# A transform-and-MLP kernel on one core: another order of loads, fillers and weight preparation in its opening

## The chip, the core and the metric

The kernel runs on one core of a Trainium2 chip. The core has a matrix engine (TensorE, PE; its weight loads are shown apart as PEld), a vector engine (VectorE, DVE), a scalar engine (ScalarE, ACT), a general engine (GpSimd, POOL) and a queue engine that only issues transfers (SyncE, SP). Transfers run on 16 DMA engines that SP, ACT and POOL feed through queues of their own. The metric is the device time of one execution in microseconds (us), the median over the runs.

## The reference

The input x has 8 entries of 3136 tokens of 256 features. Each entry is filtered along its tokens in the frequency domain, and each resulting token goes through a two-layer block with a softmax gate and a layer norm:

```python
X = np.fft.rfft(x, axis=1)                      # x: (8, 3136, 256)
y = np.fft.irfft(X * (filt_r + 1j * filt_i)[None], n=3136, axis=1)
x = y.reshape(25088, 256)
h = x @ w_in                                    # w_in: (256, 1024), float64 in memory
e = np.exp(h - h.max(-1, keepdims=True))
solu = h * (e / (e.sum(-1, keepdims=True) + 1e-09))
ln = (solu - solu.mean(-1, keepdims=True)) / np.sqrt(solu.var(-1, keepdims=True) + 1e-6) * g_ln
out = ln @ w_out                                # w_out: (1024, 256), float64 in memory
```

The two weights are float64 in memory; the kernel loads their words and turns them into float32 by integer operations.

## The kernel before

**The transform.** The 3136 tokens of an entry are 49 rows of 64. The transform along the 49 rows is a product with a small table (`first`, or `first_quarters` for later entries), in 8 pieces of 4 columns and their 4 mirror columns; then comes the transform along the 64 columns, the product with the filter, and the way back along the 64 columns, in 7 units (`forward`, `multiply`, `inverse`); then the way back along the rows (`back` for entry 0, `back_halves` for the others), which writes the tile `y` that the block reads. Entries 1 to 7 go through DRAM buffers `d1` and `d2` between these parts (`store_first`, `fetch`, `store`, `fetch_back`), and share the filter in `f_dram`.

**The opening.** Entry 0 stays on the chip. Its rows and mirrored rows are loaded into `rows_x` (L530): the first half of the partitions from SP, the second from POOL, with the four raw halves of `w_in` (`begin`, L521) between them on POOL's queue. SP then has the tables (L478), the filters (L485), small tables, six pieces of entry 1 (L473, into a part of `y` not yet used), the raw `w_out` (L425), and the stores of the filters to `f_dram` (L558). PE starts with 14 products that only keep it busy (`warm`), then 8 pieces of the row transform (L568), which ACT copies back to `rows_x` (L571). DVE converts three halves of `w_in` (`convert`, L444 to L458, nine instructions each), then turns the rows in place by four 32x32 transposes (`turn_rows`, L590). PE meanwhile does filler products (`idle`, L576) and turns the tables (`tables_back`, L498), and then the units run: `forward` on PE (L318), four multiplications on DVE (L339, L340), two additions on POOL (L341), a filler and `inverse` on PE (L576, L318), copies on ACT (L357). A second `turn_rows` follows, with six fillers beside it, then `back` (L410, copies on ACT L414), while DVE converts the last half of `w_in` and forms sums of weight blocks (`weight_sums`, L162).

**The steps.** After the opening the order is written out by hand, step after step: `step(k)` for k from 0 to 204, each with one half of a pair of 128-token blocks. A pair of blocks takes seven products with `w_in` (`product`, L755; a Strassen-like scheme over 2x2 blocks, whose sums POOL makes in `pair_sums`), which ACT and DVE bring out of PSUM (`keep`, L765; `finish`, L776 and L779), exponential, gate, turn and square (`exponential` L789, `normalize` L801, `turn` L819, `square` L809), and from step 9 on seven products with `w_out` (`project`, L891). Each engine does its instructions in the order in which they are written, so an instruction that waits holds up all that stands behind it on its engine. `PLAN` lists in which step each piece, unit and way back of entries 1 to 7 is done beside this:

```python
    ([0, 0, 0, 0, 1, 1, 1, 1], [4, 5, 6, 7, 8, 10, 12], [16, 17, 18, 19, 20, 20, 21, 22]),
```

is the line of entry 1: the first list gives the steps of its 8 pieces, the second those of its 7 units. At the end of a step come the preparation of `w_out` and the jobs in `late` and `loads`:

```python
        if k == 0:
            prepare_w_out(0)
        if k < 2:
            for n in range(2 * k, 2 * k + 2):
                convert_w_out(n)
        if k == 2:
            prepare_w_out(1)
        if k == 3:
            for n in range(2, 7):
                prepare_w_out(n)
```

`convert_w_out(n)` converts one quarter of `w_out` on DVE (nine instructions on 128x512) and scales it on ACT by `g_ln` (L682, four instructions). `prepare_w_out` takes the mean over the rows on PE (L700, 32 products), subtracts it on DVE (L705, 4) and forms the sums of blocks (L162, 4).

Of the kernel before, what the change touches and what calls it, by code (L numbers as in the profile page):

```python
# [52 lines left out]
def dft_tables():  # L53
# [19 lines left out]
    for a, part, sign in ((0, 0, 1), (1, 1, -1), (2, 1, 1), (3, 0, 1)):  # L73
# [18 lines left out]
    wb[:, :NK // 2] = wi[:, :, 0].reshape(NS, 2, 2, N1).transpose(2, 0, 1, 3).reshape(2, NK // 2, N1)  # L92
    wf0 = np.zeros((2, 64, 4, 32))
    wi0 = np.zeros((4, 32, NR))
    wf0[:, :N1, :, :NS] = wf.transpose(0, 1, 3, 2)
    wi0[:, :NS] = wi.reshape(NS, 4, NR).transpose(1, 0, 2)
    return wf.reshape(NR, NK).astype(f32), wf0.reshape(P, P).astype(f32), wq.reshape(P, 2, 64).astype(f32), \
        (-wi0).reshape(P, NR).astype(f32), (-wb).reshape(P, N1).astype(f32), de.astype(f32)
# [3 lines left out]
def kernel(  # L102
# [326 lines left out]
    with ExitStack() as st:  # L429
# [105 lines left out]
        wf0_t = fpool.tile([P, P], FP32, name="wf0_t", tag="wf0")  # L535
        nc.sync.dma_start(out=wf0_t, in_=wf0_dram)
        nc.scalar.dma_start(out=one, in_=one_dram)
        pieces = NH // NCH

        for i in range(pieces):  # L540
            fetch_x(0, NCH * i, NCH, 0, 64, nc.sync.dma_start)
            fetch_x(1, NCH * i, NCH, 0, 64, nc.gpsimd.dma_start if i else nc.scalar.dma_start)
            if i % 2:
                begin((0, 2, 1, 3)[i // 2], nc.gpsimd.dma_start)
        for load in (load_tables, load_filters):
            for i0, n in ((0, 4), (4, 4), (8, NP - 8)):
                load(i0, n, nc.sync.dma_start)
        nc.sync.dma_start(out=wi_t, in_=wi_dram)
        nc.sync.dma_start(out=wf_t, in_=wf_dram)
# [3 lines left out]
        fetch_second()  # L553
        for n in range(4):
            load_w_out(n, nc.sync.dma_start)
# [6 lines left out]
        for j in range(14):  # L562
            nc.tensor.matmul(out=ps_t.tile([P, P], FP32, name=f"warm_{j}", tag="t"), lhsT=one, rhs=one,
                             start=True, stop=True)
        for i in range(pieces):
            ps = ps_h.tile([P, 2, 512], FP32, name=f"pa_0_{i}", tag="h")
            for j in range(2):
                nc.tensor.matmul(out=ps[:, j], lhsT=wf0_t,  # L568
                                 rhs=rows_x[:, NCH * i + 2 * j:NCH * i + 2 * j + 2, :],
                                 start=True, stop=True)  # L570
            nc.scalar.copy(out=pairs_x[:, 2 * i:2 * i + 2].rearrange("p a c t -> p a t c"),  # L571
                           in_=ps.rearrange("p a (t c) -> p a t c", t=2))

        def idle(out):

            nc.tensor.matmul(out=out, lhsT=tables[0][0][:, 0, 0].rearrange("p u q -> p (u q)"),  # L576
                             rhs=filters[0][0][:, 0], start=True, stop=True)

        def idle_row(count, name):
            for j in range(count):  # L580
                idle(ps_h.tile([P, 2, C], FP32, name=f"{name}_{j}", tag="h"))

# [40 lines left out]
        turn_rows()  # L623
        convert(3)
# [50 lines left out]

    def convert_w_out(n):
        i, h, _ = quarters[n]
        power = pools["p"].tile([P, 512], I32, name=f"power_{n}", tag="pt")
        load_float64(w_out_sb[:, i].rearrange("p k d -> p (k d)"), raw_out[:, n], power)
        for f in range(KF // 2):  # L680
            fg = KF // 2 * h + f
            nc.scalar.activation(out=w_out_sb[:, i, f], in_=w_out_sb[:, i, f], func=AFT.Copy,  # L682
                                 scale=g_sb[:, fg:fg + 1])

    mean = {}

    def prepare_w_out(step):


        if step == 0:  # L690
            for name in ("ones", "w_bar"):
                mean[name] = pools["p"].tile([P, C], FP32, name=name, tag="pr" if name == "ones" else "pi")
            nc.vector.memset(mean["ones"][:, 0:P], 1.0)
            nc.vector.tensor_scalar(out=g_sb, in0=g_sb, scalar1=-1.0 / SHRINK, scalar2=None, op0=ALU.mult)
        elif step == 1:
# [239 lines left out]
    for e in range(1, B):  # L935
        first_at, spectrum_at, back_at = PLAN[e]
        sp = Spectrum(e, pools, load_filter, load_de)
        if e == 1:
            sp = second
            sp.load, sp.load_de = load_filter, load_de  # L940
        for i, t in enumerate(first_at):
            dma = nc.gpsimd.dma_start
            if e == 1:
# [56 lines left out]
    def step(k):  # L1000
# [94 lines left out]
        else:  # L1095
# [44 lines left out]
        for job in late[k] + loads[k]:  # L1140
            job()

    with tc.manual_schedule():
# [36 lines left out]
```

## Time and profile before

| what | value |
|---|---|
| median of 3 runs | 1608.41 us (1607.35 to 1610.21) |
| the profiled execution, its own time | 1609.97 us |
| its span in the profile | 1608.2 us |
| PE busy | 1555.3 us, 97% of the span |
| DVE busy | 1258.9 us, 78% |
| POOL busy | 1141.3 us, 71% |
| ACT busy | 924.7 us, 58% |
| data moved | 299.07 MB, mean 186 GB/s |

The span is the time from the first to the last instruction of the profiled execution; 1.8 us of its own time lie around it. A line of a timeline has the start, the duration, the engine, the source line, the operation with output and inputs, the count and, in brackets, how long the engine had been idle before it and what ended that. "PEq", "SPq" and the like are the sequencers that issue.

### The profile page before, as it was taken

The numbers are of one execution on the slowest core, as the hardware profiler recorded it, in microseconds if no ns is written. First come the engines' busy times: TensorE is split into PE (matmuls) and PEld (weight loads), VectorE is DVE, ScalarE is ACT, GpSimd is POOL, SyncE is SP. The second block draws the span as 40 slices with busy tenths as digits, with TensorE's granted clock in tenths as the row PEclk, the third lists the DMA queues.
The fourth block names the chain that finished last, engine by engine and source line by source line (L and its number), as shares of the span: only waits on it lengthen the run. The fifth ranks groups of instructions, "written<-read, shape, count | busy, mean of one in ns | idle before, by whom it ended". The sixth has DMA issues, their size and how long they took to land. (4 is left out here: it accounts for less than half of the span.)

```text
span 1608.2 us, 36683 instructions
## 1 busy us (share of the span) xinstructions
PE 1555.3 (97%) x12848; PEld 1066.7 (66%) x12848; DVE 1258.9 (78%) x2241; ACT 924.7 (58%) x1886; POOL 1141.3 (71%) x1338
## 2 busy tenths in 40 slices
PE   7976999999999999999999999999999999999997
PEld 3543466666666677667776677667766777777777
DVE  5655786898798888986888778986888777777773
ACT  2244565566565665665556655666656666666663
POOL 1432887679878877796788877697776766676765
PEclk8987999999999999999999999999999999999999
DMA  9624877887788678866897678766775454343444
GB/s 260 202 82 148 246 224 211 219 238 199 214 248 260 183 202 248 225 187 172 223 251 206 173 192 240 218 186 174 217 223 140 123 135 122 102 114 91 117 105 116
DMA packets 341128, 299.07 MB, mean 186 GB/s; under 512 B 28064, under 2 KB 310184, under 8 KB 340946
## 3 DMA queue, kind: packets, MB, share of 16 engines
q1 hardware_dynamic: 275026, 169.84, 39.9%
q0 software_dynamic: 31456, 93.53, 19.4%
q10 hardware_dynamic: 34464, 33.36, 7.1%
q8 instruction: 104, 1.70, 0.5%
q14 instruction: 78, 0.64, 0.1%
HBM read 119.02 MB, written 74.84 MB: 121 GB/s over the span
## 5 line engine op out<-in xcount | busy, mean ns | idle before, releaser
L891 PEld LDWEIGHTS o<-w_out_sb,solu_t 128*128 128x128 f32 x3136 | 382.7, 193 | 49.1 <-issue 43.5
L755 PE MATMUL m<-w_in_sb,s 128*128 128x512 f32 x784 | 402.0, 614 | 5.8 <-DVE nmax L779 3.4
L891 PE MATMUL o<-w_out_sb,solu_t 128*128 128x128 f32 x3136 | 401.6, 276 | 2.9 <-DVE ot L911 2.6
L891 PEld LDWEIGHTS o<-w_out_sb,u 128*128 128x128 f32 x2352 | 307.1, 192 | 138.4 <-issue 110.5
L891 PE MATMUL o<-w_out_sb,u 128*128 128x128 f32 x2352 | 310.9, 276 | 2.2 <-POOL u L734 1.6
L755 PE MATMUL m<-w_in_sb,y 128*128 128x512 f32 x588 | 308.5, 608 | 2.3 <-DVE h L776 2.3
L801 DVE SCALAR_TENSOR_TENSOR h<-e,h 128x1024 f32<-128x1024 f32 x196 | 307.8, 1570 | 0.0
L765 ACT COPY h<-m 128x512 f32<-128x512 f32 x294 | 173.0, 588 | 202.6 <-PE m L755 195.7
L907 ACT ACTIVATE ot<-o,rs_t 128x128 f32<-128x128 f32 x392 | 143.2, 367 | 245.7 <-PE o L891 244.1
L779 DVE CUSTOM_DVE_ANT_0 h<-m,h 128x512 f32<-128x512 f32 x196 | 134.3, 685 | 191.7 <-ACT h L765 112.7
L734 POOL TENSOR_TENSOR u<-solu_t 128x512 f32<-128x512 f32 x98 | 133.6, 1363 | 183.6 <-DMA solu_t<-turn 112.2
L809 ACT ACTIVATE h<-h,nmu 128x1024 f32<-128x1024 f32 x196 | 224.9, 1147 | 48.7 <-DVE turn L819 48.7
L819 DVE STREAM_TRANSPOSE turn<-h 128x1024 f32<-128x1024 f32 x196 | 243.1, 1240 | 3.1
L789 ACT ACTIVATE e<-h,nmax 128x1024 f32<-128x1024 f32 x196 | 225.3, 1149 | 6.9 <-DVE h L801 5.5
L734 POOL TENSOR_TENSOR u<-solu_t,u 128x512 f32<-128x512 f32 x98 | 136.0, 1388 | 93.8 <-PE o L891 93.5
L755 PEld LDWEIGHTS m<-w_in_sb,s 128*128 128x128 f32 x784 | 129.0, 192 | 93.5 <-issue 73.1
L911 DVE SCALAR_TENSOR_TENSOR ot<-o,rs_t,ot 128x128 f32<-128x128 f32 x299 | 103.7, 347 | 98.5 <-ACT ot L907 56.4
L734 POOL TENSOR_TENSOR u<-u,solu_t 128x512 f32<-128x512 f32 x98 | 160.2, 1634 | 15.2 <-PE o L891 8.3
L755 PEld LDWEIGHTS m<-w_in_sb,y 128*128 128x128 f32 x588 | 98.0, 193 | 97.5 <-issue 53.0
L734 POOL TENSOR_TENSOR solu_t<-solu_t,solu_t 128x512 f32<-128x512 f32 x98 | 156.1, 1593 | 0.9
L734 POOL TENSOR_TENSOR s<-y 128x128 f32<-128x128 f32 x196 | 96.2, 491 | 26.5 <-ACT y L414 26.0
L387 PEld LDWEIGHTS py<-wb_t,t 50*64 50x64 f32 x3584 | 57.6, 135 | 43.1 <-issue 18.7
(124 smaller groups left out, 1968.5 us busy)
## 6 DMA issues: line engine op xcount, KB each, us to landing
solu_t<-turn SPq DMA_DIRECT2D x780, 128.0 KB
out_dram<-ot SPq DMA_DIRECT2D x196, 128.0 KB
t<-d POOLq DMA_DIRECT2D x112, 200.0 KB, 6.8
d<-x POOLq DMA_DIRECT2D x100, 200.0 KB, 5.1
f<-f_dram POOLq DMA_DIRECT2D x39, 512.0 KB, 7.7
t<-d ACTq DMA_DIRECT2D x37, 512.0 KB
d<-g POOLq DMA_DIRECT2D x36, 512.0 KB, 5.1
x<-in_x_dram SPq DMA_DIRECT2D x112, 98.0 KB
```

What stands on the lines that cost most here:

```text
L387: nc.tensor.matmul(out=views[g][64 * h:64 * h + 64, cb, i, :], lhsT=t4[rows, i, c0:c0 + 64], rhs=wb_t[rows, 0:N1], start=True, stop=True)
L734: nc.gpsimd.tensor_tensor(out=out, in0=in0, in1=in1, op=op)
L755: nc.tensor.matmul(out=ms[j, bank], lhsT=lhsT, rhs=w_in_sb[:, w, :], start=m in (1, 2, 7), stop=True, skip_group_check=True)
L765: nc.scalar.copy(out=h_half(k, i), in_=ms[j, 0])
L779: nc.vector.tensor_tensor_reduce(out=h_half(k, i), in0=ms[j, bank], in1=h_half(*kept), scale=1.0, scalar=sofar, op0=ALU.add, op1=ALU.min, ...
L789: nc.scalar.activation(out=e, in_=hs[k], func=AFT.Exp, bias=nmaxs.pop(k)[:, 1:2], scale=-1.0, accum_out=esums[g][:, i:i + 1])
L801: nc.vector.scalar_tensor_tensor(out=solu, in0=e, scalar=SHRINK, in1=solu, op0=ALU.mult, op1=ALU.mult, accum_out=nmu)
L809: nc.scalar.activation(out=solu, in_=solu, func=AFT.Square, bias=nmu, scale=-float(DFF), accum_out=variances[g][:, i:i + 1])
L819: nc.vector.transpose(out=turns[g][:, :, i, :], in_=solus[k].rearrange("p (f j) -> p f j", j=32))
L891: nc.tensor.matmul(out=pos[p, bank], lhsT=lhs[:, f, :], rhs=w[:, f, :], start=f == 0 and (m in (1, 2, 7) or alone), stop=True, skip_group_ ...
L907: nc.scalar.activation(out=out_half(p, *to)[0], in_=pos[p, 0], func=AFT.Copy, scale=rs)
L911: nc.vector.scalar_tensor_tensor(out=ot, in0=pos[p, bank], scalar=rs, in1=out_half(p, *kept)[0], op0=ALU.mult, op1=ALU.add)
```

## The change

The opening and the first seven steps are put in another order; the computation is the same. The changed parts:

- The first table has 98 rows, not 128, and the rows of x stand on 98 partitions: 48 of the first half (SP), 49 of the second (POOL; its first piece is 48 rows and one more from ACT), and the 49th row of the first half apart, in two pieces. Before, 64 rows were loaded for each half.
- ACT's queue has the first piece of the second half and the raw halves 0 and 2 of `w_in`; halves 1 and 3 go to SP's queue behind the filters. Tables and filters alternate. The pieces of entry 1 come ahead of the small tables, the raw `w_out` behind the stores to `f_dram`. `one` goes to the end of POOL's queue.
- 10 `warm` products with the first table, not 14 with `one`. The fillers are 128x128 products of `one`: eight ahead of each group of tables. The fillers in the units and beside the second turn are gone.
- Only two halves of `w_in` are converted ahead of the first turn; the other two follow the second turn.
- The last unit's additions are on DVE, not POOL. The last copy of the row transform is made in two halves.
- Pieces 0 to 2 of entry 1 are done beside the second turn (`EARLY`), pieces 3 to 5 in step 0, and 6 and 7 in step 1.
- One quarter of `w_out` is converted in each of steps 0 to 3, in two halves of 128x256, and scaled by ACT one step later. The mean is in step 5, subtraction and sums in step 6; the two small tiles of the mean lie in `raw_out`.

```diff
+EARLY = 3
-    ([0, 0, 0, 0, 1, 1, 1, 1], [4, 5, 6, 7, 8, 10, 12], [16, 17, 18, 19, 20, 20, 21, 22]),
+    ([0] * 6 + [1] * 2, [4, 5, 6, 7, 8, 10, 12], [16, 17, 18, 19, 20, 20, 21, 22]),
...
-            dma(out=rows_x[64 * h + r0:64 * h + r0 + rows, n0:n0 + n],
+            to = NR - 1 if r0 else (N1 - 1) * h
+            dma(out=rows_x[to:to + rows, n0:n0 + n],
...
-        nc.scalar.dma_start(out=one, in_=one_dram)
+        fetch_x(1, 0, NCH, 0, N1 - 1, nc.scalar.dma_start)
+        fetch_x(0, 0, NH // 2, N1 - 1, 1, nc.scalar.dma_start)
+        nc.scalar.dma_start(
+            out=rows_x[NR - 2:NR - 1, 0:NCH][:, ::-1],
...
+        begin(0, nc.scalar.dma_start)
+        begin(2, nc.scalar.dma_start)
+        nc.scalar.copy(out=small_consts[:, 5:6], in_=small_consts[:, 0:1])
         for i in range(pieces):
-            fetch_x(0, NCH * i, NCH, 0, 64, nc.sync.dma_start)
-            fetch_x(1, NCH * i, NCH, 0, 64, nc.gpsimd.dma_start if i else nc.scalar.dma_start)
-            if i % 2:
-                begin((0, 2, 1, 3)[i // 2], nc.gpsimd.dma_start)
-        for load in (load_tables, load_filters):
-            for i0, n in ((0, 4), (4, 4), (8, NP - 8)):
+            fetch_x(0, NCH * i, NCH, 0, N1 - 1, nc.sync.dma_start)
+            if i == pieces // 2 - 1:
+                fetch_x(0, NH // 2, NH // 2, N1 - 1, 1, nc.sync.dma_start)
+            if i:
+                fetch_x(1, NCH * i, NCH, 0, N1, nc.gpsimd.dma_start)
+        nc.gpsimd.dma_start(out=one, in_=one_dram)
+        for i0, n in ((0, 4), (4, 4), (8, NP - 8)):
+            for load in (load_tables, load_filters):
                 load(i0, n, nc.sync.dma_start)
+        begin(1, nc.sync.dma_start)
+        begin(3, nc.sync.dma_start)
...
-        for j in (0, 2, 1):
+        for j in (0, 2):
             convert(j)
-        idle_row(3, "idle")
         for i0, n in ((0, 4), (4, 4), (8, NP - 8)):
+            idle_row(8, f"idle_{i0}")
             tables_back(i0, n)
-            idle_row(2, f"idle_{i0}")
         turn_rows()
...
-            sp.multiply(i, 0, nc.gpsimd.tensor_tensor)
-            sp.multiply(i, 1, nc.gpsimd.tensor_tensor)
+            add = (nc.gpsimd if i + 1 < units else nc.vector).tensor_tensor
+            sp.multiply(i, 0, add)
+            sp.multiply(i, 1, add)
...
-            idle(pss[0])
...
-        idle_row(6, "idler")
+        turn_rows()
+        for i in range(EARLY):
+            for u in range(2):
+                second.first(i, (u,), ps_t.tile([P, 2, C], FP32, name=f"pa_1_{i}_{u}", tag="t").rearrange(
...
+                second.store_first(i, 2 * u, nc.gpsimd.dma_start)
...
-        turn_rows()
+        convert(1)
         convert(3)
...
         if k == 0:
+            nc.vector.tensor_scalar(out=g_sb, in0=g_sb, scalar1=-1.0 / SHRINK, scalar2=None, op0=ALU.mult)
+        if k < 4:
+            for half in range(2):
+                convert_w_out(k, half)
+        if k == 4:
             prepare_w_out(0)
-        if k < 2:
-            for n in range(2 * k, 2 * k + 2):
-                convert_w_out(n)
-        if k == 2:
+        if k == 5:
             prepare_w_out(1)
-        if k == 3:
+        if k == 6:
             for n in range(2, 7):
                 prepare_w_out(n)
         for job in late[k] + loads[k]:
             job()
+        if 0 < k < 5:
+            scale_w_out(k - 1)
```

In the changed kernel the lines of the steps are some 22 higher: `product` is L777, `finish` L798 and L801, `project` L913, the row transform of entry 0 L582, its turn L605, `forward` and `inverse` L320, the conversions L446 to L460, the scaling L706.

More of the change, by code (lines that the diff above doesn't have):

```diff
@@ L92, in dft_tables @@
     wb[:, :NK // 2] = wi[:, :, 0].reshape(NS, 2, 2, N1).transpose(2, 0, 1, 3).reshape(2, NK // 2, N1)
[L93 removed]
+    wf0 = np.zeros((2, N1, 4, 32))
     wi0 = np.zeros((4, 32, NR))
[L95 removed]
+    wf0[:, :, :, :NS] = wf.transpose(0, 1, 3, 2)
+    wf0 = wf0.reshape(NR, P)[np.r_[0:N1 - 1, N1:NR, N1 - 1]]
     wi0[:, :NS] = wi.reshape(NS, 4, NR).transpose(1, 0, 2)
[L97 removed]
+    return wf.reshape(NR, NK).astype(f32), wf0.astype(f32), wq.reshape(P, 2, 64).astype(f32), \
         (-wi0).reshape(P, NR).astype(f32), (-wb).reshape(P, N1).astype(f32), de.astype(f32)
@@ L560 @@
                 in_=f[0:rows, at:at + n].rearrange("p i k c -> p i (k c)"))
-        for j in range(14):
-            nc.tensor.matmul(out=ps_t.tile([P, P], FP32, name=f"warm_{j}", tag="t"), lhsT=one, rhs=one,
+        for n in range(4):
+            load_w_out(n, nc.sync.dma_start)
+        for j in range(10):
+            nc.tensor.matmul(out=ps_t.tile([P, P], FP32, name=f"warm_{j}", tag="t"), lhsT=wf0_t, rhs=wf0_t,
                              start=True, stop=True)
@@ L568 @@
                 nc.tensor.matmul(out=ps[:, j], lhsT=wf0_t,
-                                 rhs=rows_x[:, NCH * i + 2 * j:NCH * i + 2 * j + 2, :],
+                                 rhs=rows_x[0:NR, NCH * i + 2 * j:NCH * i + 2 * j + 2, :],
                                  start=True, stop=True)
-            nc.scalar.copy(out=pairs_x[:, 2 * i:2 * i + 2].rearrange("p a c t -> p a t c"),
-                           in_=ps.rearrange("p a (t c) -> p a t c", t=2))
+            size = 2 if i < pieces - 1 else 1
+            for j in range(0, 2, size):
+                nc.scalar.copy(out=pairs_x[:, 2 * i + j:2 * i + j + size].rearrange("p a c t -> p a t c"),
+                               in_=ps[:, j:j + size].rearrange("p a (t c) -> p a t c", t=2))
         def idle(out):
-            nc.tensor.matmul(out=out, lhsT=tables[0][0][:, 0, 0].rearrange("p u q -> p (u q)"),
-                             rhs=filters[0][0][:, 0], start=True, stop=True)
+            nc.tensor.matmul(out=out, lhsT=one, rhs=one, start=True, stop=True)
         def idle_row(count, name):
             for j in range(count):
-                idle(ps_h.tile([P, 2, C], FP32, name=f"{name}_{j}", tag="h"))
+                idle(ps_h.tile([P, P], FP32, name=f"{name}_{j}", tag="h"))
         def convert(j):
@@ L674, in load_filter, with convert_w_out, scale_w_out @@
         return f
-    def convert_w_out(n):
+    def convert_w_out(n, half):
+        i = quarters[n][0]
+        part = slice(256 * half, 256 * half + 256)
+        power = pools["p"].tile([P, 256], I32, name=f"power_{n}_{half}", tag="pt")
+        load_float64(w_out_sb[:, i].rearrange("p k d -> p (k d)")[:, part], raw_out[:, n, part], power)
+    def scale_w_out(n):
         i, h, _ = quarters[n]
-        power = pools["p"].tile([P, 512], I32, name=f"power_{n}", tag="pt")
-        load_float64(w_out_sb[:, i].rearrange("p k d -> p (k d)"), raw_out[:, n], power)
         for f in range(KF // 2):
@@ L683, in convert_w_out @@
                                  scale=g_sb[:, fg:fg + 1])
-    mean = {}
+    mean = {name: raw_out[:, n].rearrange("p k w -> p (k w)").bitcast(FP32)[:, 0:C]
+            for n, name in enumerate(("ones", "w_bar"))}
     def prepare_w_out(step):
         if step == 0:
-            for name in ("ones", "w_bar"):
-                mean[name] = pools["p"].tile([P, C], FP32, name=name, tag="pr" if name == "ones" else "pi")
             nc.vector.memset(mean["ones"][:, 0:P], 1.0)
-            nc.vector.tensor_scalar(out=g_sb, in0=g_sb, scalar1=-1.0 / SHRINK, scalar2=None, op0=ALU.mult)
         elif step == 1:
@@ L941 @@
         for i, t in enumerate(first_at):
+            if e == 1 and i < EARLY:
+                continue
             dma = nc.gpsimd.dma_start
```

12 lines of the change are left out of this document (7 added, 5 removed).

## The prediction

> **What bounds the kernel now.** I read the page's slices first, then the busy time of each engine by stage, then the timeline of the stages that are not full.
>
> The slices (40.2 us each; tenths of PE's busy time and of its granted clock):
>
> ```profile
> PE   7976999999999999999999999999999999999997
> PEclk8987999999999999999999999999999999999999
> ```
>
> PE has holes only in the first four slices. The stage view (edges chosen at: turn starts, first forward matmul, units done, step 0, step 4, step 9) says how much:
>
> ```profile
> core 0: us, PE busy (x) PEld busy (x) DVE busy (x) ACT busy (x) POOL busy (x), PEclk, DMA share, GB/s
> 0.00:32.40 32.40, 22.67 (x60) 11.88 (x60) 13.94 (x30) 9.95 (x9) 7.06 (x15) 0.89 0.98 257
> 32.40:46.40 14.00, 12.38 (x44) 6.89 (x44) 8.88 (x4) 1.93 (x4) 0.00 (x0) 0.88 0.89 218
> 46.40:70.80 24.40, 22.38 (x217) 11.50 (x217) 15.94 (x29) 7.19 (x13) 16.24 (x14) 1.00 0.86 287
> 70.80:90.50 19.70, 19.70 (x140) 16.94 (x139) 15.90 (x17) 7.28 (x15) 0.00 (x0) 1.00 0.03 10
> 90.50:143.30 52.80, 35.27 (x94) 14.97 (x93) 26.11 (x56) 21.31 (x45) 17.92 (x34) 0.81 0.40 121
> 143.30:189.40 46.10, 38.84 (x206) 15.09 (x206) 38.11 (x67) 23.48 (x44) 28.41 (x31) 0.87 0.73 201
> 189.40:1608.20 1418.80, 1404.05 (x12096) 989.39 (x12092) 1139.99 (x2041) 853.58 (x1757) 1071.70 (x1245) 1.00 0.67 187
> ```
>
> From 189.4 on PE is busy 1404 of 1419 us and the change leaves that code alone; I carry this stage over whole. All that can move lies before it. The first stage is full of DMA (0.98). In 32.4 to 70.8 PE looks busy, but partly with fillers; these timeline rows show them on the path:
>
> ```profile
> 32.39 8.89 DVE L590 STREAM_TRANSPOSE x<-x 128x2048 f32<-128x2048 f32 x4 [3.30 <-ACT x L571]
> ...
> 44.59 1.88 PE L576 MATMUL idle<-f,de 128*128 128x512 f32 x4
> ...
> 46.41 3.06 PE L318 MATMUL pb<-x,de 64*64 64x256 f32 x48
> ...
> 65.60 1.13 PE L576 MATMUL pc<-f,de 128*128 128x512 f32 x2 [0.78 <-ACT x L357]
> ...
> 70.80 8.89 DVE L590 STREAM_TRANSPOSE x<-x 128x2048 f32<-128x2048 f32 x4 [7.10 <-ACT x L357]
> ```
>
> The turn ends at 41.28, yet the forward products start at 46.41, when fillers and the turned tables are through. In steps 0 to 3 (52.8 us with 35.3 of PE) the stall has this form:
>
> ```profile
> 124.59 0.69 DVE L458 TENSOR_TENSOR w_out_sb<-w_out_sb,raw_out 128x512 f32<-128x512 f32 x1
> ...
> 125.32 1.28 ACT L682 ACTIVATE w_out_sb<-w_out_sb,g_sb 128x128 f32<-128x128 f32 x4 [3.43 <-DVE w_out_sb L458]
> 126.50 1.04 ACT L245 COPY y<-pa 100x512 f32<-100x512 f32 x2
> ...
> 127.12 3.73 PE L243 MATMUL pa<-x,wf_t 98*100 98x512 f32 x4 [10.34 <-ACT y L245]
> ...
> 133.75 0.69 DVE L779 CUSTOM_DVE_ANT_0 h<-m,h 128x512 f32<-128x512 f32 x1 [8.46 <-PE m L755]
> ```
>
> DVE converts two quarters, ACT waits in its queue to scale them, the evacuations stand behind the scaling, PE waits for the evacuations, and then DVE waits 8.46 us for PE. The same loop ran at 98 to 110 (7.12 us).
>
> **The change part by part.**
>
> *Loads and first turn.* Ahead of the turn come 32 K of x per row: 98 rows, not 128, so 3.2 MB for 4.2; and two raw weights (1.05 MB), not three or four (1.6 to 2.1). About 2.0 MB less at the stage's 257 GB/s is 7.8 us. A second bound: x and weights are now on three queues, all done near 4.4 MB / 257 GB/s + 2.2 us = 19.3; the second raw weight lands at 18.5 to 19 and its conversion (9 instructions, 4.74 us in the timeline, 19.54 to 24.28) must be done before DVE can turn: 23.5. The last ACT copy, now in two halves, is done by 22. So the turn goes 23.5 to 32.4: 8.9 earlier.
>
> The 49-row pieces on POOL are the doubtful part. Between 41 and 50 us only 49-row loads (y from x, SP) run, and the windows give DMA share 0.50 and 146 GB/s, against 1.12 and 289 in 28 to 40. A 49-row piece may thus take twice as long alone; on POOL they share engines with two other queues, so I price this 0 to 3 us and take 0.
>
> The Trainium skill (DMA: Bandwidth & Descriptors, "Why a DMA increments its semaphore by 16 and not by 1") says that a copy runs on the largest number of engines up to 16 that divides its slowest dimension: 7 for 49 rows, 16 for 48. The share of 0.50 agrees on SP; by it the seven POOL pieces, if serial at half of 146 GB/s (19.2 us for 1.4 MB), would end 2 us later, and the sum would be 1576.5.
>
> *Fillers before the products.* Three rows of eight 128x128 fillers replace nine 128x512 ones. A 128x128 product takes 0.26 (the `back` rows, 4 in 1.05), so a row is 2.1 and lies between table arrivals. Tables and filters now alternate: 7.4 MB precede the last table, landed at 29.5 to 31; 5 products more give 31 to 32.3. That is beside the turn. `one`, which fillers and tables need, is last on POOL's queue, near 20. Forward starts at 32.5, not 46.4: 13.9, of which 8.9 is the turn and 5.0 the fillers. If the last table were late, each us counts: 0 to 3.
>
> *Units.* Each filler in a unit waits for ACT and costs 0.86 on PE: the last units are 2.95 apart. Without it POOL's two additions (1.28 each) are the limit, and the last unit's additions move to DVE (0.4 each). POOL's first addition starts 2.6 after the forward; 12 at 1.24 end at +17.5; inverse 1.1, copies 1.1 and the short last unit end at +20.1, not +24.4: 4.3 gained, units done at 52.6.
>
> *Pieces 0 to 2 of entry 1.* 12 passes of 0.43 = 5.2 us of PE, six copies of 0.58 on ACT, six stores on POOL (0.54 each), in place of 5.4 us of fillers, under the 8.9 us turn. The next products need half of the turn (4.45): start at +4.7, before +4.6. Cost 0.1. Their loads come behind filters and two raw weights, about 9.5 MB by 39 us; three pieces at 146 GB/s land by 47, needed at 52. Step 0 then starts at 52.6 + 4.7 + 15.2 = 72.5, before 90.5: **18.0 gained**.
>
> *Conversions 1 and 3*, their raw weights now on SP behind the filters (landed by 39), run on DVE after the turn, 61.5 to 71.0; sums 2.6 to 73.6; the first two products need neither, so about 0.3 of cost.
>
> *Output weights.* They are last on SP's queue behind f_dram's stores. In the old trace y, w_out and f_dram took from 40.7 to about 71; they now start at 39, so the first quarter lands near 64, needed at 75: hidden, with 10 us to spare. Scaling one step later takes ACT's wait away. DVE becomes the limit: from 73.6 to the end of step 4's first `finish` it has 9 finishes (0.75), 2 normalizes (1.22), one turn (1.24) and four quarters. A quarter takes 4.79 now (120.49 to 125.28); in halves, between 4.79 and 5.9, by 64x256 rows at 0.40 against 0.68 for 128x512; I take 5.4, the middle. Sum 32.1, so 105.7; where DVE still waits for PE (step 0 to 1 and the three finishes of step 1, one slow matmul after a 4 us hole in step 3) I add 4.2: 109.9. Before, this instruction ended at 150.65: 40.7 earlier, **22.7 beyond the opening**.
>
> *Moved.* The old 150.65 includes the mean (32 matmuls, 3.7 us on PE) and the subtraction and sums (2.5 + 2.6 on DVE). These now stand in steps 5 and 6, after my point, where DVE is busy 38 of 46 us; its waits there (0.8 and 1.8 before finishes) hide some 2: **6.8 lost**. POOL's early stores stand ahead of `pair_sums`, which waits for y anyway: 0.
>
> Sum: 18.0 + 22.7 - 6.8 = 33.9. The profiled execution took 1609.97 with a span of 1608.2; its span becomes 1574.3. Against the median of the runs, 1608.41, that is **1574.5 us**.
>
> **Rivals.**
>
> 1. *Smaller gain.* The four quarters on DVE hold PE as the ACT chain did: `finish` of each step stands behind a conversion and the next products need the bank it frees. If steps 0 to 4 give only half (11), and the moved work costs its full 8.8: 1608.4 - 18 - 11 + 8.8 = 1588. For it: DVE is the limit in my own sum. Against: 15.6 us of DVE idling (7.12 and 8.46) had a cause that goes.
>
> 2. *Slower, by a cold PE.* Fillers leave, and PE waits for DVE in each step. The trace: 512-column matmuls run at 0.43 after a 2.1 us hole and at 0.85 after 2.75 (34.02), 5.84 and 10.34. If holes of over 2.5 us came in every stage, the py products (15.1) would take 30, and the 56 us of PE work in steps 0 to 8 would take 112: step 9 at 72.5 + 15 + 112 = 199.5, not 189.4, 1618. It decides once PE's time at half clock passes DVE's in a step. Against: I find one such hole, in step 3; units leave at most 1.4.
>
> The Trainium skill (TensorE: Matmul & The Clock Gate, Part 1) has the clock halve after an idle window of about 3.4 us; the 2.75 row here is shorter than that, so the trace is stricter.
>
> 3. *No effect.* Steps 7 and 8 move data at a DMA share of 1.0; if these transfers, not the engines, set when step 9 begins, the gain is lost in waiting: 1608. Against: they are issued by steps, so they move along.
>
> **How the numbers follow.** Forecast 0.81, smaller gain 0.11, slower 0.05, no effect 0.03. Range: from 1565 (DVE never idle in steps 0 to 4, -4.2; moved work hidden, -4; opening 1.5 better) to 1588 (rival 1; also tables 3, x 3 and quarters of 5.9 late). About 0.2% is what a measurement here can tell from none. Faster 0.92, same 0.03, slower 0.05.
>
> **What would show it.** Right: turn near 23.5, first `pb` near 32.5, units 2.5 apart, first L777 product near 72.5, no ACT wait on `w_out_sb` ahead of evacuations, step 9 near 155.5, and the rest unchanged at about 1419. Wrong: `pb` waiting for a table or POOL's x; DVE waiting for `raw_out`; PEclk near 0.5 in steps 0 to 8; the stage after step 9 longer than 1419.

## The result, and the profile after

The changed kernel takes **1587.03 us** in the median (1585.0 to 1591.0), beside 1609.31 for the kernel before (1607.35 to 1611.18); the ratio is 0.9865, with a 95% interval of 0.9842 to 0.9888. The forecast was 1574.5, with a range of 1565 to 1588. The direction was right and the range held the time, but of the 33.9 us that the sum promised only some 22 came.

The profiled execution took 1591.0 us (span 1589.2), the slowest of its four. First the page's slices (39.7 us each), in tenths:

```profile
PE   7968999999999999999999999999999999999997
PEclk9998999999999999999999999999999999999999
```

They hardly differ from those before: the holes are still in the first slices, and what was gained is gained inside them. The view by stages has the same events as edges (turn starts, first forward product, units done, step 0, step 4, step 9):

```profile
core 0: us, PE busy (x) PEld busy (x) DVE busy (x) ACT busy (x) POOL busy (x), PEclk, DMA share, GB/s
0.00:29.40 29.40, 22.00 (x63) 12.62 (x64) 9.27 (x20) 10.31 (x11) 6.24 (x12) 1.00 0.88 213
29.40:38.50 9.10, 7.33 (x68) 7.16 (x68) 8.89 (x4) 1.93 (x4) 0.00 (x0) 1.00 0.98 271
38.50:59.00 20.50, 17.38 (x202) 11.88 (x202) 17.59 (x30) 7.20 (x13) 14.89 (x12) 1.00 0.66 231
59.00:78.90 19.90, 19.90 (x140) 16.49 (x139) 19.52 (x25) 10.82 (x22) 3.35 (x6) 1.00 0.78 269
78.90:110.00 31.10, 22.71 (x51) 8.27 (x50) 25.94 (x74) 15.28 (x30) 14.94 (x28) 0.92 0.57 168
110.00:162.70 52.70, 42.51 (x239) 18.99 (x238) 45.18 (x86) 25.62 (x53) 28.25 (x30) 0.85 0.67 191
162.70:1589.20 1426.50, 1405.79 (x12096) 988.29 (x12092) 1126.19 (x2041) 853.70 (x1759) 1067.48 (x1246) 1.00 0.68 185
```

The first stage shrank from 32.4 to 29.4 only, at 213 GB/s instead of 257. The stage from the turn to the first forward product went from 14.0 to 9.1, the units from 24.4 to 20.5, steps 0 to 3 from 52.8 to 31.1. Steps 4 to 8 grew (46.1 to 52.7), and so did the long last stage, from 1418.8 to 1426.5, though PE is busy in it for only 1.7 us more. The timeline of the changed kernel, PE's and DVE's rows at these points:

```profile
12.04 16.19 PE L582 MATMUL pa<-x,wf_t 98*128 98x512 f32 x32 [4.50 <-DMA x<-in_x_dram]
...
25.45 0.69 DVE L460 TENSOR_TENSOR w_in_sb<-w_in_sb,raw 128x512 f32<-128x512 f32 x1
...
29.43 8.89 DVE L605 STREAM_TRANSPOSE x<-x 128x2048 f32<-128x2048 f32 x4 [3.29 <-ACT x L587]
...
38.47 3.05 PE L320 MATMUL pb<-x,de 64*64 64x256 f32 x48 [1.77 <-DVE x L605]
...
59.03 8.89 DVE L605 STREAM_TRANSPOSE x<-x 128x2048 f32<-128x2048 f32 x4 [1.68 <-ACT x L359]
...
108.08 4.85 PE L777 MATMUL m<-w_in_sb,y 128*128 128x512 f32 x6 [4.20 <-DVE nmax L801]
```

The first row is the finding of the opening. The 32 passes of the row transform (`pa`) wait until 12.04 for x, after an idle time of 4.50, and take 16.19 us, 0.51 each; before, they started at 8.14. (The clock has no record before 16.5 us in this trace, and a PEclk of 1.00 there means nothing. The weight loads of the passes stand 0.85 us apart until 16.47 and 0.43 from then on: PE began cold, at half speed.) What they wait for is the smallest of the new loads: row 48 of the first mirrored piece, 4 KB in four packets, issued on ACT's queue at 3.69 and complete, by the trace's semaphore events, at 12.0. The second row is the end of DVE's second conversion, at 26.14. The turn, the third row, waits for ACT, which copies behind these passes. The fourth row names `x` from the turn, no longer fillers or tables: the fillers left the path as meant. The last row is a wait of PE for a `finish` of DVE that stands behind conversions, in steps 0 to 4.

### The profile page after: what moved, and what is told of

It reads as the page before. It is cut to its first block, busy times and chain, and to the rows that moved or that the text cites. A ratio compares the mean times of both kernels' runs of the same rounds, so it can differ in the third digit from the quotient of the medians.

```text
span 1589.2 us, 36720 instructions
## 1 busy us (share of the span) xinstructions
PE 1537.6 (97%) x12844; PEld 1063.7 (67%) x12844; DVE 1252.6 (79%) x2279; ACT 924.8 (58%) x1888; POOL 1135.1 (71%) x1333
## 4 chain that ended last, share of the span: by engine, by line
PE 81%; DMA 9%; DVE 4%; POOL 2%; issue 1%; SPq 1%; ACT 0%; ACTq 0%; POOLq 0%; DVEq 0%
PE m L777 34%; PE o L913 33%; PE py L389 4%; DMA solu_t<-turn 4%; DMA x<-in_x_dram 3%; PE pc L320 3%; PE pb L320 3%; PE pa L288 2%; PE py L412 1%; DMA f<-in_filt_r_dram 1%; PE pa L245 1%; SPq L858 1%; POOL u L756 1%; DMA de<-de_tbl 1%; DMA t<-d 1%
## 5 line engine op out<-in xcount | busy, mean ns | idle before, releaser
L913 PEld LDWEIGHTS o<-w_out_sb,solu_t 128*128 128x128 f32 x3136 | 381.2, 192 | 48.7 <-issue 43.3
L777 PE MATMUL m<-w_in_sb,s 128*128 128x512 f32 x784 | 400.0, 611 | 12.3 <-DVE nmax L801 6.5
L913 PE MATMUL o<-w_out_sb,solu_t 128*128 128x128 f32 x3136 | 400.2, 276 | 3.1 <-DVE ot L933 2.4
L913 PEld LDWEIGHTS o<-w_out_sb,u 128*128 128x128 f32 x2352 | 307.6, 192 | 139.1 <-issue 108.2
L777 PE MATMUL m<-w_in_sb,y 128*128 128x512 f32 x588 | 311.1, 613 | 9.5 <-DVE nmax L801 8.0
L913 PE MATMUL o<-w_out_sb,u 128*128 128x128 f32 x2352 | 310.8, 276 | 2.0 <-POOL u L756 1.4
L823 DVE SCALAR_TENSOR_TENSOR h<-e,h 128x1024 f32<-128x1024 f32 x196 | 296.5, 1513 | 0.0
L756 POOL TENSOR_TENSOR u<-solu_t 128x512 f32<-128x512 f32 x98 | 136.8, 1396 | 205.2 <-DMA solu_t<-turn 105.3
L801 DVE CUSTOM_DVE_ANT_0 h<-m,h 128x512 f32<-128x512 f32 x196 | 134.3, 685 | 185.6 <-ACT h L787 101.1
L777 PEld LDWEIGHTS m<-w_in_sb,s 128*128 128x128 f32 x784 | 128.2, 191 | 99.9 <-issue 76.1
L777 PEld LDWEIGHTS m<-w_in_sb,y 128*128 128x128 f32 x588 | 97.6, 193 | 106.1 <-issue 46.6
L756 POOL TENSOR_TENSOR u<-u,solu_t 128x512 f32<-128x512 f32 x98 | 152.6, 1557 | 15.0 <-PE o L913 7.4
L756 POOL TENSOR_TENSOR solu_t<-solu_t,solu_t 128x512 f32<-128x512 f32 x98 | 151.5, 1546 | 0.9
L756 POOL TENSOR_TENSOR s<-y 128x128 f32<-128x128 f32 x196 | 100.4, 512 | 14.7 <-ACT y L416 14.3
```

What stands on the lines that cost most here:

```text
L756: nc.gpsimd.tensor_tensor(out=out, in0=in0, in1=in1, op=op)
L777: nc.tensor.matmul(out=ms[j, bank], lhsT=lhsT, rhs=w_in_sb[:, w, :], start=m in (1, 2, 7), stop=True, skip_group_check=True)
L801: nc.vector.tensor_tensor_reduce(out=h_half(k, i), in0=ms[j, bank], in1=h_half(*kept), scale=1.0, scalar=sofar, op0=ALU.add, op1=ALU.min, ...
L823: nc.vector.scalar_tensor_tensor(out=solu, in0=e, scalar=SHRINK, in1=solu, op0=ALU.mult, op1=ALU.mult, accum_out=nmu)
L913: nc.tensor.matmul(out=pos[p, bank], lhsT=lhs[:, f, :], rhs=w[:, f, :], start=f == 0 and (m in (1, 2, 7) or alone), stop=True, skip_group_ ...
```

## The experiments

Each run is compared with the kernel before on its own chip. Ratios carry their 95% intervals; a difference of two medians from different chips is only a guide.

**48-row pieces on POOL.**

```diff
-                fetch_x(1, NCH * i, NCH, 0, N1, nc.gpsimd.dma_start)
+                fetch_x(1, NCH * i, NCH, 0, N1 - 1, nc.gpsimd.dma_start)
+                if i == 1:
+                    last_row(1, NH // 2 - NCH)           # row 48, columns 4 to 15
+                    last_row(NH // 2 // NCH, NH // 2)    # row 48, columns 16 to 31
```

> The changed kernel, with the seven 49-row pieces of x on POOL's queue cut to 48 rows; their 49th row comes in two single-row loads behind the second piece. Theory A (a 49-row piece is slow: it landed last, at 24.86 us, and the turn started at 29.43 instead of 23.5): the last piece lands near 20, the turn starts between 23.5 and 26.1 (VectorE was free at 26.14), time 1581 to 1584 us, against 1587. Rival B (a row loaded by itself is the slow one, as the first product waited for one until 12.04): the two new single rows land as late, the turn starts at 29 or later, time 1587 or more. Rival C (three queues share the engines and order alone decides): within 1 us of the changed kernel.

1584.83 us, ratio 0.9848 (0.9829 to 0.9867): no difference from the changed kernel that can be measured. The transfers of the first 30 us, with KB each and median us from issue to landing, in the changed kernel and then in this one:

```profile
x<-in_x_dram POOLq DMA_DIRECT2D x7, 196.0 KB, 14.7
```

```profile
x<-in_x_dram POOLq DMA_DIRECT2D x7, 192.0 KB, 10.4
```

The pieces did land 4.3 us sooner, and the last one at 21.85 instead of 24.86. Yet the turn started at 29.97, for the first pass started at 11.90 (12.04). The reversed row of the first piece, still on ACT's queue, was complete at 11.9. Theory A had the right price and the wrong place: POOL's pieces were not what ended last. The Trainium skill (DMA: Bandwidth & Descriptors, "Why a DMA increments its semaphore by 16 and not by 1"), by which 49 rows run on 7 engines and 48 on 16, agrees with the two landings and says nothing about the turn. The landings (14.7 and 10.4 us) do not show the engines themselves.

**64+64 rows.**

```diff
-            fetch_x(0, NCH * i, NCH, 0, N1 - 1, nc.sync.dma_start)
+            fetch_x(0, NCH * i, NCH, 0, 64, nc.sync.dma_start)
-                fetch_x(1, NCH * i, NCH, 0, N1, nc.gpsimd.dma_start)
+                fetch_x(1, NCH * i, NCH, 0, 64, nc.gpsimd.dma_start)
...                                    # no loads of single rows; wf0_t with 128 rows
```

> The changed kernel with x loaded as before, 64 rows for each half on two queues (128 rows, 4.2 MB and no rows by themselves), all else changed. Theory A (fewer bytes bring the turn forward, as in the prediction's sum): 1 MB more at 257 GB/s, the turn 3.9 us later than 29.4, time near 1591. Rival B (48+49+1 rows lose by their form what they save in bytes): the turn at 26 to 29, time 1584 to 1587, so that this part of the change brings nothing.

**1580.27 us**, ratio 0.9809 (0.9791 to 0.9826), an interval that lies wholly below that of the changed kernel: rival B, and by more than it said. With 1 MB more to load, the turn starts at 25.53. The passes in its timeline:

```profile
7.14 2.26 PE L574 MATMUL pa<-x,wf_t 128*128 128x512 f32 x4
11.04 1.96 PE L574 MATMUL pa<-x,wf_t 128*128 128x512 f32 x4 [1.64 <-DMA x<-in_x_dram]
13.80 10.54 PE L574 MATMUL pa<-x,wf_t 128*128 128x512 f32 x24 [0.80 <-DMA x<-in_x_dram]
```

The first pass starts at 7.14 and 24 of the 32 run in 10.54 us (0.44 each) with no wait. One more difference stands in the windows from 12 to 16 us, the changed kernel's first, then this one's:

```profile
12.00:16.00 4.00, 3.96 (x5) 1.85 (x6) 0.00 (x0) 0.14 (x1) 0.00 (x0) 1.00 1.05 262
```

```profile
12.00:16.00 4.00, 3.20 (x8) 1.22 (x7) 3.83 (x9) 1.32 (x2) 0.00 (x0) 1.00 1.02 340
```

At a full DMA share (1.05 and 1.02) this kernel, with 128 partitions, moves 340 GB/s, and the changed one, with 98, 262: a quarter fewer bytes at a quarter less speed. The kernel before, with 128 partitions and another order of loads, had 286 in this window, so the partitions are not all that sets the rate.

**All single rows on POOL's queue.**

```diff
-        fetch_x(0, 0, NH // 2, N1 - 1, 1, nc.scalar.dma_start)
-        nc.scalar.dma_start(...)                          # row 48 of the first mirrored piece
+        fetch_x(0, 0, NH // 2, N1 - 1, 1, nc.gpsimd.dma_start)
+        last_row(0, NCH)
```

(With the 48-row pieces, and the other two halves behind the second piece on POOL.)

> The changed kernel, with 48-row pieces on POOL's queue and all rows that come by themselves taken from ACT's and SP's queues to the head of POOL's (there two of them landed 6.4 us after issue in the run with 48 rows, while the others landed at 12.8 and 21.5). Theory A (TensorE's 32 passes, 13.8 us at full clock, start only at 12.04 because the single row on ACT's queue is late): the first pass starts near 7 to 8, as with 64+64 rows (7.14), the turn at 24 to 26, time 1581 to 1583. Rival B (the 96 or 98 partitions themselves are filled more slowly, 235 GB/s at a DMA share of 1.0 where 128 partitions got 300): x is complete no earlier than 20, the raw weights land behind it, and the turn stays at 28 or later, time 1585 to 1587.

(The landings of 12.8 and 21.5 in this text were misread: the semaphore events give 4.6 and 11.8 for the two 16 KB rows of the changed kernel, and 12.0 for the 4 KB row. That a row by itself, on ACT's queue, holds the first pass stands.)

1586.52 us (1580.88 to 1587.64), ratio 0.9841 (0.9817 to 0.9864). Between the two: the 4 KB row, issued at 2.01, is complete at 10.14, the first pass starts at 10.23, neither at 8 nor at 12, and the turn at 27.09. Its window from 12 to 16 us shows why the passes still took 15.67:

```profile
12.00:16.00 4.00, 4.00 (x8) 1.67 (x7) 3.83 (x9) 1.48 (x2) 1.78 (x3) 0.71 1.02 258
```

PE had idled 2.61 us between its warm-up products and the first pass, and the granted clock is 0.71. The Trainium skill (TensorE: Matmul & The Clock Gate, Part 1) puts the idle window at about 3.4 us. Here 2.61 was enough, as 2.75 was in the trace before. But the length of the hole alone does not decide: later in this same trace PE idled for 2.71 us and went on at full clock, four matmuls in 1.96 us:

```profile
98.09 1.96 PE L783 MATMUL m<-w_in_sb,s 128*128 128x512 f32 x4 [2.71 <-DVE nmax L807]
```

**98 rows in a better order.**

```diff
-        begin(2, nc.scalar.dma_start)
+                if i == 5:
+                    begin(2, nc.sync.dma_start)           # behind the sixth piece of x
-        for j in range(10):
+        for j in range(18):                               # warm-up products
```

(On top of the kernel of the last run, with whole quarters of the output weights, as below.)

> The run with all single rows on POOL's queue, with three edits more: the second raw weight is loaded on SP's queue behind the sixth piece of x instead of ahead of it on ACT's, 18 warm-up products stand before the first pass instead of 10, and quarters of the output weights are converted whole. Theory A (98 rows can start the turn as early as the prediction said, once x comes first and TensorE stays warm): first pass by 9.5 at full clock (13.8 us for the 32 passes, 15.7 without), turn at 23.5 to 25, time 1577 to 1580. Rival B (98 partitions fill too slowly, or VectorE's second conversion is now last): turn at 26 or later, time 1582 or more.

1581.29 us, ratio 0.9821 (0.98 to 0.9842).

```profile
10.04 1.88 PE L589 MATMUL pa<-x,wf_t 98*128 98x512 f32 x4
12.75 1.96 PE L589 MATMUL pa<-x,wf_t 98*128 98x512 f32 x4 [0.82 <-issue]
14.88 10.57 PE L589 MATMUL pa<-x,wf_t 98*128 98x512 f32 x24 [0.17 <-DMA x<-in_x_dram]
...
25.48 1.13 ACT L594 COPY x<-pa 128x512 f32<-128x512 f32 x2 [0.64 <-PE pa L589]
...
26.64 8.89 DVE L612 STREAM_TRANSPOSE x<-x 128x2048 f32<-128x2048 f32 x4 [4.85 <-DMA f<-in_filt_r_dram]
```

PE stayed warm (0.44 a pass) and all of x had landed by 21.4, 4.0 us before the passes end, and still the turn is no earlier than 26.64; DVE idled 4.85 ahead of it. (The last row names a load of the filters, but the turn needs ACT's copies, and the last of them, the row above it, end at 26.61.) So the turn is not set by when the last byte comes, but by a chain: the first pass (10.04), 15.4 us of passes and their waits, and 1.2 us to the end of ACT's copy. The 4 KB row was complete at 8.9 here and my 18 warm-up products lasted until 10.04, so by this sum the best this order could give is some 1.1 us less: 25.5, where 64+64 rows start. The smaller load brings the turn no earlier: x was complete at 21.4 here and at 20.1 in the run before, and at 21.2 with 64+64 rows.

**Whole quarters of the output weights.**

```diff
-            for half in range(2):
-                convert_w_out(k, half)
+            convert_w_out(k)                              # nine 128x512 instructions
```

> The changed kernel with each quarter of the output weights converted whole (nine 128x512 instructions), not in two halves, at the same places. Theory A (VectorE is the limit of steps 0 to 4): four quarters at 4.8 instead of 6.2 us take 5.6 us off, step 9's first product near 157 instead of 162.7, time near 1581.5. Rival B (VectorE then waits for TensorE instead, which has holes and half clock there): step 9 earlier by 2 us at most, time 1585 or more.

1584.67 us, ratio 0.9841 (0.9824 to 0.9859), 2.4 us below the changed kernel in the median, but the two intervals overlap. Last quarter in each, first and last instruction of the nine (changed kernel, two halves):

```profile
112.01 0.29 DVE L446 TENSOR_SCALAR raw_out<-raw_out 128x256 int32<-128x256 int32 x1
...
117.63 0.43 DVE L460 TENSOR_TENSOR w_out_sb<-w_out_sb,raw_out 128x256 f32<-128x256 f32 x1
```

and this kernel:

```profile
111.00 0.42 DVE L446 TENSOR_SCALAR raw_out<-raw_out 128x512 int32<-128x512 int32 x1
...
115.11 0.69 DVE L460 TENSOR_TENSOR w_out_sb<-w_out_sb,raw_out 128x512 f32<-128x512 f32 x1
```

6.05 us in halves, 4.80 whole. Over the four quarters about 5 us of DVE went (25.3 to 20.2). From step 0 to step 9 the trace has 80.7 us instead of 83.8, so 3.1 of the 5 arrived in the time of these steps. That is less than theory A said and more than rival B.

**The output weights alone, and the opening alone.** First, the kernel before with only the new schedule:

```diff
-        if k < 2:
-            for n in range(2 * k, 2 * k + 2):
-                convert_w_out(n)                          # and scale it at once
+        if k < 4:
+            convert_w_out(k)
...                                    # mean in step 5, subtraction in step 6
+        if 0 < k < 5:
+            scale_w_out(k - 1)
```

> The kernel before, with the schedule of the output weights alone taken from the change: one whole quarter in each of steps 0 to 3, scaled one step later, the mean in step 5 and the subtraction in step 6. Theory A (this part brings what the two traces show between step 0 and step 9, 98.9 us before and 83.8 after): 15 to 20 us faster, 1589 to 1594, step 9 near 171 to 174. Rival B (the gain of these steps needs the earlier opening too, because loads are then out of the way): under 8 us faster, over 1601.

1595.13 us (1594.15 to 1598.94), ratio 0.9909 (0.9894 to 0.9925): 15.9 us below its own before, theory A. Then the changed kernel with that diff undone:

> The changed kernel, with the output weights converted, scaled and averaged in steps 0 to 3 as before (two whole quarters in each of steps 0 and 1, scaling at once), so that only the opening is changed. Theory A (the parts add): the opening brought step 0 forward by 11.6 us, so the time is 1598 to 1600, and with 15.6 us from the output weights the two make up 26, more than the 22 to 24 measured together. Rival B (the parts overlap): 1602 to 1604, the rest of the opening's 11.6 us being lost behind step 0 even without the new schedule.

1595.56 us, ratio 0.9896 (0.9875 to 0.9916), 15.0 us below. Both theories missed. Each part alone is worth 15 to 16 us, and the changed kernel 20 to 22. That does not show a gain paid twice, because both parts were run with whole quarters and the changed kernel has halves. The two parts put together are the run with whole quarters, 26.3 us below its own before: some 5 us less than the 30.9 of the parts, hardly clear of the intervals. In the traces step 9 starts at 189.4 before, at 176.5 with the schedule alone, at 176.7 with the opening alone and at 160.6 with both: 12.9 and 12.8 us alone, 28.8 together. Up to step 9 the parts add; what is missing is lost behind it.

**No early pieces.** `EARLY = 3` becomes `EARLY = 0`.

> The changed kernel with pieces 0 to 2 of entry 1 back in steps 0 and on, none in the second turn. Theory A (VectorE limits steps 0 to 4, so TensorE can take the pieces' 5.2 us there): within 2 us of the changed kernel, 1585 to 1589. Rival B (the second turn leaves TensorE idle for 4.5 us, the py products start cold, and the steps carry the pieces): py longer by 3 us or more and step 9 later by 5 to 10, time 1592 to 1597. If the wait for x in steps 42 to 48 (6.4 us lost there) comes from the early pieces, that loss goes, and the stage after step 9 is near 1419.

1594.02 us (1589.73 to 1603.33), ratio 0.9888 (0.9863 to 0.9912). That is rival B in size, though its interval overlaps that of the changed kernel; the trace has the mechanism:

```profile
65.47 17.10 PE L412 MATMUL py<-wi_t,x 128*128 128x98 f32 x128 [5.14 <-issue]
...
84.15 5.44 PE L245 MATMUL pa<-y,wf_t 98*100 98x512 f32 x12
```

PE idles 5.14 us under the second turn, the `py` products take 17.10 instead of 15.30, and the passes of six pieces stand between the first products of the steps, 10.9 us (a second group of twelve follows at 91.14), where the changed kernel has 5.6.

**Fillers back.**

```diff
-            nc.tensor.matmul(out=out, lhsT=one, rhs=one, start=True, stop=True)
+            nc.tensor.matmul(out=out, lhsT=tables[0][0][:, 0, 0].rearrange("p u q -> p (u q)"),
+                             rhs=filters[0][0][:, 0], start=True, stop=True)
...                                    # rows of 128x512 behind each table, three before the first
+            idle(pss[0])                                  # one in each unit
```

> The changed kernel with the fillers of before put back: 128x512 products behind each group of turned tables, three before the first, and one in each unit. Theory A (prediction: 5.0 us of the forward start and 4.3 us of the units): forward start 0 to 5 later than 38.5 (the turn ends at 38.3 now, so part of the fillers may lie beside it), units 24.4 instead of 20.6, time 1591 to 1596. Rival B (fillers keep the clock up and cost nothing): time 1587 or less.

1591.16 us, ratio 0.9878 (0.9855 to 0.9902). That is theory A's time, though the interval overlaps that of the changed kernel; the trace shows the mechanism. Its units take 24.38 us (39.85 to 64.23) instead of 20.56, while the fillers ahead of the forward products cost only 0.6: beside a turn that ends at 38 to 39 they are hidden.

**The changed kernel again.**

> The changed kernel itself, once more. Theory A (the 6.4 us lost in steps 42 to 48 and the 7.7 us lost in the whole stage after step 9 belong to the change): the stage is again 1424 us or longer, time near 1587. Rival B (they belong to the one profiled execution, the slowest of its four): the stage is 1419 to 1421 and the profiled time near 1583.

1590.61 us (1584.33 to 1593.16), ratio 0.9864 (0.984 to 0.9888), the same as the first time. The stage after step 9 is long again (span 1591.3):

```profile
162.30:1591.30 1429.00, 1403.37 (x12096) 987.44 (x12092) 1142.72 (x2041) 854.14 (x1759) 1065.03 (x1246) 1.00 0.67 185
```

Theory A: the loss after step 9 came twice. But the profiled execution is again the slowest of its group, so how much of it the others have is not known.

**The two better edits together, and a version beyond them.** 64+64 rows with whole quarters:

> The changed kernel with 64+64 rows of x and whole quarters, the two edits that were faster than the changed kernel alone (by 6.7 and 2.3 us in the medians). Theory A (one lies before step 0, the other behind it, so they add): 1578. Rival B (with the earlier opening VectorE waits for TensorE in steps 0 to 4 and the whole quarters bring nothing): 1580 to 1581.

**1579.27 us** (1572.15 to 1582.45), ratio 0.98 (0.9775 to 0.9825). It beats both kernels, but in time whole quarters add nothing that can be told from 64+64 rows alone (0.9809). The traces do tell it: step 0 to step 9 takes 79.8 us here and 85.5 with halves. So rival B's reason, that DVE would then only wait for PE, does not hold. In the last version two conversions were moved into DVE's idle time as well:

```diff
+        begin(1, nc.scalar.dma_start)
-        for j in (0, 2):
+        for j in (0, 2, 1):
             convert(j)
...
+        load_float64(w_out_sb[:, quarters[0][0]]..., raw_out[:, 0], ...)    # ahead of step 0
...
-        if k < 4:
-            convert_w_out(k)
+        if k < 3:
+            convert_w_out(k + 1)
```

> The changed kernel with 64+64 rows and whole quarters, and two conversions moved into VectorE's idle time: raw weight 1 is loaded on ACT's queue and converted ahead of the first turn (VectorE waited 6.15 us there), and the first quarter of the output weights is converted before step 0, the other three in steps 0 to 2. Theory A (VectorE limits steps 0 to 4): 4.8 us less in them, step 9 earlier by 3 to 5 than with the two edits alone, time 1574 to 1576 (1579.3 without). Rival B (the third raw weight delays x, or the quarter's load is late, or TensorE limits these steps by now): 1578 or more.

1584.38 us, ratio 0.9826 (0.9802 to 0.9849): rival B. The third raw weight moved the turn from 25.94 to 27.20, and a piece of entry 1 now came too late:

```profile
90.70 3.71 PE L245 MATMUL pa<-x,wf_t 98*100 98x512 f32 x4 [3.56 <-DMA x<-in_x_dram]
```

PE waited 3.56 us and ran the passes cold (0.93 each, 3.71 us for what took 1.88 in the changed kernel). That is about the 4.8 us taken off DVE; step 0 to step 9 takes 81.1 us.

## Why the prediction was right in sign and short by 12 us

The steps of the sum against the profiled execution (forecast span 1574.3, measured 1589.2):

| step | forecast | measured | us lost |
|---|---|---|---|
| first turn starts | 23.5 | 29.43 | 5.9 |
| turn to first forward product | 9.0 | 9.04 | 0.0 |
| units | 20.1 | 20.56 | 0.5 |
| units done to step 0 | 19.9 | 19.88 | 0.0 |
| step 0 to the end of step 4's first `finish` | 37.4 | 39.75 | 2.4 |
| from there to step 9 | 45.6 | 44.06 | -1.5 |
| from step 9 on | 1418.8 | 1426.5 | 7.7 |

**The first turn** is one of the two terms that failed. The prediction worked out when bytes arrive (19.3) and when DVE has converted (23.5), and booked the last ACT copy at 22. That holds only if the passes start near 8, as before. They started at 12.04, cold after 4.50 us of idling: 12.04 + 16.19 + 1.2 gives 29.43. DVE's bound failed as well: the first raw weight was there only at 16.6, and the second conversion ended at 26.14, not 23.5. So without the late passes the turn would have come at 26.14 at best: they alone account for 3.3 of the 5.9. Both premises of its byte count failed too: the rate was 213 GB/s, not 257, and POOL's last piece landed at 24.86 (early enough for the last passes). The doubt it did name, 49-row pieces, was real in the landings and worth nothing in the time. That the late 4 KB row delays the first pass is read from its completion (12.0, 11.9 and 10.14 in three kernels, with the first pass at 12.04, 11.90 and 10.23) and from the run without such rows. In all seven kernels with this row on ACT's queue it is complete between 11.9 and 12.9, and the first pass starts within 0.05 us of that. Why four packets need 8.3 us, while a 16 KB row issued ahead of them on the same queue was complete 3.4 us after issue, stays open.

**Fillers, units, early pieces** went as written. The fillers ahead of the forward products were less of a gain by themselves than the 5.0 booked, since the late turn hides them now. The early pieces were booked as a cost of 0.1; that was right as far as it went, but if they had not been moved, 5.4 us of passes would have stood in step 0 and `py` would have started cold.

**Output weights.** 15.9 was forecast for step 0 to step 9, and 15.1 came; the schedule alone took 13.1 off these steps of the kernel before, and 15.9 off its time. Within it, a quarter in halves cost 6.05 to 6.5 us, above the upper bound of 5.9: 25.3 for the four, where the sum took 21.6. DVE's waits came to 4.3 us, as booked (4.2). The 3.7 us of the quarters, less 1.3 in small items, are the 2.4; the moved mean and subtraction cost 5.3, not 6.8.

**The later stage** was carried over whole, and this is the other term that failed: it was put at no change, and measured 7.7 us longer. The loss is densest in steps 36 to 48, where the DMA share is 0.8 to 1.0. Between the `normalize` instructions (L823) of these two steps lie 98.8 us in the kernel before and 98.9 with the output weights alone, but 100.5 to 105.3 in all twelve profiles with a changed opening (100.9 with 64+64 rows and whole quarters, 103.8 with the opening alone, 102.1 without early pieces). PE's waits in steps 42 to 48, in the changed kernel:

```profile
PE pa L288 <- POOL x L279: 2.6, 2, 2.2
PE m L777 <- ACT h L787: 1.6, 2, 1.4
```

Before, one wait of 0.2 us stood there. In the second profile of the changed kernel the 2.2 us wait is absent and others stand in its place, so no one wait is the cause. That the loss in steps 36 to 48 comes with the changed opening is shown, by two profiles against twelve that do not overlap. For the whole stage it is less clear: 1416.5 and 1418.8 us with the old opening, 1418.5 to 1430.9 with a changed one. Which part of the opening does it is open; the early pieces, the output weights and the 98 rows are excluded as its only cause. Of the 7.7, some 4 may be this execution, since the other three of the first comparison had spans 4 to 6 us shorter.

**The rivals.** The smaller gain (1588) came out in time, but not by its mechanism. PE did wait for DVE's `finish` behind the conversions, 14.1 us in four waits of steps 0 to 8, but the sum had priced DVE as the limit: only 2.4 us were lost there, not 11. That the range held the time is in part luck. Its upper end was this rival's, the time lies 1 us below it, and the repeat of the same kernel, at 1590.61, lies above it. The cold PE of the second rival is real: in the first passes, in `py` without early pieces, and in steps 3 to 8, where the prediction had found one hole and the clock fell to half three times, after holes of 4.20, 3.79 and 3.40 us (the PEclk of 0.92 and 0.85 in the stages). It stays far from the 1618 of that rival. The third did not come: step 9 moved by 26.7 us.

## What to carry to other kernels

A stage that is full of transfers ends with a chain, not with its last byte: write down the first usable piece, the work that must pass through one engine after it, and the copy behind that, before counting bytes saved. Do not count bytes saved by loading fewer partitions as time saved: here x was complete some 1 us sooner at best. A tiny transfer that the first product needs is worth more care than the bulk. Parts of a change should be tried alone and together, in the same form, and compared at a marked point of the trace as well as in the whole time.

## What the runs showed of the hardware

From 12 to 16 us, at a DMA share of 1.02 to 1.06, the nine kernels that load x into 98 partitions moved 253 to 279 GB/s, and the five that load it into 128, the kernel before among them, 286 to 340. Their orders of loads differ too, so that the partitions are the cause is not shown. A 4 KB row in four packets was complete 8.3 us after issue among this traffic. PE ran cold after idling for 2.61 us, and at full clock after 2.71 in the same trace. A conversion in two 128x256 halves cost 6.05 us, whole 4.80: the same elements in twice the instructions were 26% dearer.
